# Attention with a max of three products: later differences over blocks of the units, and the softmax scaled on DVE

## The chip, the cores and the metric

The kernel runs on one core of one Trainium2 chip. The metric is device microseconds (us) of one execution. A measurement is repeated, and the median of the runs is given. The engines are TensorE (PE, with its weight loads shown apart as PEld), VectorE (DVE), ScalarE (ACT), GpSimd (POOL) and SyncE (SP). Each works through its own queue in order, and waits for the others by semaphores. DMAs are issued from the queues of SP, ACT and POOL.

## The reference, cut to what matters

```python
batch, n_heads, seq, head_dim = (8, 8, 576, 64)
scores = scale * np.matmul(q, k.transpose(0, 1, 3, 2))
mask = (rel >= 0) & (rel < 128)                      # a window of 128 keys
scores = np.where(mask, scores + bias[None], -1000000000.0)
attn = np.exp(scores - np.max(scores, axis=-1, keepdims=True))
attn = attn / (np.sum(attn, axis=-1, keepdims=True) + 1e-09)
x = np.matmul(attn, v)                               # to 4608 tokens x 512
h = np.maximum(np.maximum(x @ w1, x @ w2), x @ w3)   # 512 -> 768, three times
out = h @ w_out                                      # 768 -> 512
```

All is float32.

## The kernel before

**Attention.** A task is one batch entry and one pair of heads; there are 32 tasks, four to a batch entry. Each goes in five steps of 128 queries (the last has 64), and the steps are taken in pairs. For a pair, `products` makes the scores on PE, `score` folds the window by a predicated copy on DVE, adds the bias and takes the least value on DVE (L289), and takes the exponential on ACT (L293), which leaves the sum of each row. `sums_of` adds 1e-9 (L302) and takes the reciprocal (L305), both on DVE and on two or four values per row. `normalise` then multiplies each 128x128 tile of the exponentials by the reciprocal of its row: four instructions for a pair of steps, two for a single one, on ACT (L312). `turn` transposes the tiles on PE (L321), ACT copies them out of PSUM (L325, L331, L334), POOL cuts two triangles (L335, L339), and `mix` multiplies by v (L361).

**The units.** The products with the weights are done as a fast matrix multiplication of 2x2 blocks by 2x2 blocks: seven products (`unit(u)`, taken in the order k = 0, 1, 6 of the group before, 2, 3, 4, 5) in place of eight. A batch entry has eleven groups of seven: nine with w1, w2, w3 (g = 0 to 8) and two with w_out (g = 9 and 10). Each operand is split into a high and a low part in float32r, and three of the four products of the parts are made, so a unit has 6 matmuls for g < 9 and 18 for g >= 9 (L510). A unit ends with a copy out of PSUM on ACT (`t`, L519) or with `put`, which adds two parts (L473, L476) and takes the maximum (L468, L474) into the tiles `hq` on DVE. Three banks of PSUM take turns.

**The differences over blocks.** Three groups make one third p of the hidden layer: four blocks b00, b01, b10, b11 in `hq`. The products with w_out need the blocks and four differences: t = b01 - b00, t' = b11 - t, b01' = b11 - b01 and b10' = b10 - t'. `factors_h` issues these (`sub`, on DVE, L391) and the splits of the results (`cut`: the high part is a copy on ACT, L387, the low part a subtraction on POOL, L388, or on DVE for two of them at p = 2). The differences are written in place, over `t`, b01 and b10. So t' waits until POOL has made the low part of t, and b10' waits until POOL has made the low part of b10.

**The order.** `later(when, what, ...)` puts a piece of work on a list, and unit number `when` issues it ahead of its own matmuls. Before, the work that a `put` of unit u calls for is issued at u + 1: for block (0,0) the splits of b00 and t; for (1,1) t', b01' and the splits of t' and b11; for (1,0) the splits of b01' and b10, then b10' and its split. The events of attention, units and the preparing of the weights are sorted by hand-written times (`at`); `normalise` stands 0.4 steps behind `sums_of`, and `turn` of that pair comes about two and a half steps later. Within one engine the trace shows small exchanges against the order of the code: at 419.94 us b01' runs ahead of t' at 421.17 us.

**The weights.** In the first 200 us or so DVE and ACT also prepare the weights (L136 to L169), and SP stores them to HBM (L171). After that POOL issues DMAs that stream them back for every batch entry, through a ring of two places (L221).

Of the kernel before, what the change touches and what calls it, by code (L numbers as in the profile page):

```python
# [12 lines left out]
AF = mybir.ActivationFunctionType  # L13
ALU = mybir.AluOpType
# [15 lines left out]
def attention_maxout_kernel(  # L30
# [11 lines left out]
    nc = tc.nc  # L42
# [43 lines left out]
        out=prev, in_=prev, pattern=[[1, P]], compare_op=ALU.is_gt, fill=0.0,  # L86
# [220 lines left out]
    def normalise(t, i):  # L307
        n = rows[i]
        st, two = stats[t, i // 2]
        for a, p in enumerate(two):  # L310
            for j in range(2):
                nc.scalar.activation(p[:n, j], p[:n, j], AF.Copy, scale=st[:n, 2, a, j:j + 1])  # L312

    def turn(s):
        pt = ps_t.tile([P, 2, 2, P], F32, name="pt")
# [63 lines left out]
    def later(when, what, *args):  # L379
        todo.append((when, what, args))  # L380
        todo.sort(key=lambda x: x[0])
# [3 lines left out]
    def split(out, src, e):  # L385
        hi, lo = out
        nc.scalar.copy(out=hi, in_=src)  # L387
        e.tensor_tensor(out=lo, in0=src, in1=hi.bitcast(F32), op=ALU.subtract)  # L388

    def sub(out, x, y):  # L390
        nc.vector.tensor_tensor(out=out, in0=x, in1=y, op=ALU.subtract)  # L391
# [28 lines left out]
    def factors_h(b, p, ij, when):  # L420
        b00, b01, b10, b11 = [hq.get((p, x)) for x in ((0, 0), (0, 1), (1, 0), (1, 1))]

        def cut(k, src):
            if p < 2:
                if p == 0:
                    hs[b, k] = hs_p.tile([P, 2, 2, C], F32R, name="hs")
                t = hs[b, k][:, p]
            else:
                if k in (0, 2, 4, 5):
                    hs[b, "at"] = hs_p.tile([P, 2, 2, C], F32R, name="hs2", bufs=4)  # L430
                t = hs[b, k, 2] = hs[b, "at"][:, k in (1, 3, 6)]
            split((t[:, 0], t[:, 1]), src, nc.vector if p == 2 and k < 2 else nc.gpsimd)

        if ij == (0, 0):
            t = hq["t", p] = t_p.tile([P, C], F32, name="t")
            sub(t, b01, b00)
            later(when, cut, 0, b00)
            later(when, cut, 1, t)
        elif ij == (1, 1):
            t = hq["t", p]  # L440
            later(when, sub, t, b11, t)
            later(when, sub, b01, b11, b01)
            later(when, cut, 2, t)
            later(when, cut, 3, b11)
        elif ij == (1, 0):
            t = hq["t", p]
            later(when, cut, 5, b01)
            later(when, cut, 4, b10)
            later(when, sub, b10, b10, t)
            later(when, cut, 6, b10)  # L450

    def put(b, g, ij, ps, e, when):
        i, j = ij
        if g >= 9:
            o = t_p.tile([P, C], F32, name="t")
            if e is None:
                nc.scalar.copy(out=o, in_=ps)
            else:
                nc.vector.tensor_tensor(out=o, in0=ps, in1=e, op=ALU.add)
            m = i * W + (g - 9) * P  # L460
            nc.sync.dma_start(outT[m:m + P, b * S + j * C:b * S + (j + 1) * C], o)
            return
        p, w = divmod(g, 3)
        if w == 0:
            hq[p, ij] = hq_p.tile([P, C], F32, name="hq")
        h = hq[p, ij]
        if w and e is None:
            nc.vector.tensor_tensor(out=h, in0=ps, in1=h, op=ALU.max)  # L468
        elif e is None:
            nc.scalar.copy(out=h, in_=ps)  # L470
        elif w:
            s = t_p.tile([P, C], F32, name="t")
            nc.vector.tensor_tensor(out=s, in0=ps, in1=e, op=ALU.add)  # L473
            nc.vector.tensor_tensor(out=h, in0=s, in1=h, op=ALU.max)  # L474
        else:
            nc.vector.tensor_tensor(out=h, in0=ps, in1=e, op=ALU.add)  # L476
        if w == 2:
            factors_h(b, p, ij, when + 1)
# [54 lines left out]
    for t, (b, hp) in enumerate(tasks):  # L533
        for i in range(NB):
            s = t * NB + i + shift[b]
            if i == LOAD_I and t + 2 < len(tasks):
                at(s - 0.4, load, t + 2)
            if i == NB - 1 and t + 1 < len(tasks):
                at(s - 0.4, load_v, t + 1)
            if i == 0 and 0 < t < NP:  # L540
                at(s - 1, slopes, t)
            c = s - (t * NB + i) % 2

            if s == c:
                at(c + LAG_T + 0.02, turn, t * NB + i)
                at(c + 0.03, products, t * NB + i)
            at(s + 0.04, score, t, i)
            if i % 2 or i + 1 == NB:
                at(s + 0.9, sums_of, t, i)
                at(s + 1.3, normalise, t, i)  # L550
            e = t * NB + next(min(e + 1, NB - 1) for e in GROUPS if e >= i)
            at(e - e % 2 + shift[b] + LAG_X + 0.01, mix, t, i)

    ready = [n_steps * (b + 1) - 2 + LAG_X + 0.05 + shift[b] for b in range(B)]
    when = ready[0]
    for b in range(B):
# [4 lines left out]
        for u in range(77 * b, 77 * b + 77):  # L561
            if u == 77 * b + 63 and b + 1 < B:
                when = max(when, ready[b + 1])
# [53 lines left out]
```

## Time and profile before

| | us |
|---|---|
| median of 3 runs (lowest, highest) | 849.85 (846.66, 851.54) |
| the profiled execution's own time | 846.03 |
| its span, first to last instruction | 844.3 |
| PE busy | 780.3 (92% of the span) |
| PEld busy | 674.3 (80%) |
| DVE busy | 570.0 (68%) |
| ACT busy | 544.5 (64%) |
| POOL busy | 310.3 (37%) |

The profiled execution is one of many: it is 3.8 us below the median of the runs. The shares are means over very different stretches. In the first 190 us attention for the first two batch entries and the preparing of the weights go side by side. From there to about 740 us a pattern repeats about every 94 us: the products of one batch entry and the attention for the next. After 740 us only products are left. A row of groups of instructions gives the line, the engine, the operation, out<-in with shapes, the count, the busy time and the mean of one in ns, and then the engine's idle time ahead of them with what ended it. In a timeline the columns are the start, the duration, the engine, the line, and in brackets how long the engine had been idle and what ended that.

### The profile page before, as it was taken

Reading aid. Unit: us, or ns where it says so; the run is one execution under the profiler, and the core shown is the slowest. Engines: PE = TensorE matmul, PEld = TensorE weight load, DVE = VectorE, ACT = ScalarE, POOL = GpSimd, SP = SyncE. Lnnn points to the kernel's source line nnn. Section 1 sums busy time; section 2 is a strip of 40 time slices with the busy share of each in tenths; the row PEclk is TensorE's granted clock in tenths of the full one; section 3 lists DMA queues with packets and bytes.
Section 4 is the critical chain, followed back from the end, with each engine's and each line's share of the span. In section 5 each row is a group of like instructions: output and inputs, shape, how many; then the busy total and the mean of one; then the engine's idle time right before and its main releaser. Section 6 shows DMA issues by size and latency. Waiting matters only on the chain.

```text
span 844.3 us, 17942 instructions
## 1 busy us (share of the span) xinstructions
PE 780.3 (92%) x6272; PEld 674.3 (80%) x6272; DVE 570.0 (68%) x1830; ACT 544.5 (64%) x1790; POOL 310.3 (37%) x544
## 2 busy tenths in 40 slices
PE   4767778799999999999999999999999999999997
PEld 2335666589888988888888988889888988889897
DVE  5788989996666845775557845775657846583552
ACT  6898888876666856676556756675657756642332
POOL 1212141442354415452345415451345415440431
PEclk9865989799999999999999999999999999999999
DMA  6742568673887558873787558873787557764851
GB/s 230 278 168 70 220 230 305 210 257 125 262 277 249 195 171 261 277 253 118 239 273 252 196 175 267 275 255 110 245 281 240 194 187 244 230 223 153 296 205 56
DMA packets 43401, 184.78 MB, mean 219 GB/s; under 512 B 4784, under 2 KB 13744, under 8 KB 34096
## 3 DMA queue, kind: packets, MB, share of 16 engines
q0 software_dynamic: 18144, 115.61, 41.7%
q1 hardware_dynamic: 25024, 67.97, 22.8%
q8 instruction: 49, 0.80, 0.4%
q14 instruction: 40, 0.33, 0.1%
q10 hardware_dynamic: 144, 0.07, 0.0%
HBM read 157.68 MB, written 25.95 MB: 217 GB/s over the span
## 4 chain that ended last, share of the span: by engine, by line
PE 68%; DVE 8%; issue 8%; POOL 6%; ACT 6%; DMA 3%; SPq 0%; POOLq 0%; ACTq 0%; DVEq 0%
PE ps_m L510 53%; PE ps_x L361 6%; PE ps_s L259 5%; PE pt L321 4%; POOL hs L388 3%; DMA wt<-keep 2%; POOL pp L339 1%; POOL pp L335 1%; ACT p L293 1%; ACT hs L387 1%; DVE hs L158 1%; DVE t L473 1%; DMA hs<-in_w_all 1%; DVE hs L144 1%; DVE xs L388 1%
## 5 line engine op out<-in xcount | busy, mean ns | idle before, releaser
L510 PE MATMUL ps_m<-xs,wt 128*128 128x288 f32 x3024 | 440.8, 302 | 19.9 <-DVE hq L476 7.6
L510 PEld LDWEIGHTS ps_m<-xs,wt 128*128 128x128 f32 x3024 | 414.6, 191 | 46.6 <-issue 12.2
L519 ACT COPY t<-ps_m 128x288 f32<-128x288 f32 x264 | 101.2, 392 | 92.3 <-PE ps_m L510 91.9
L335 POOL TENSOR_SCALAR_AFFINE_SELECT pp<-pr 128x256 f32<-128x256 f32 (+1 forms) x128 | 53.9, 421 | 263.0 <-ACT pr L334 175.9
L510 PE MATMUL ps_m<-hs,ow 128*128 128x288 f32 x1008 | 144.5, 299 | 3.2 <-POOL hs L388 2.4
L293 ACT ACTIVATE p<-s,st 128x128 f32<-128x128 f32 (+1 forms) x320 | 126.7, 399 | 27.9 <-DVE st L289 27.2
L510 PEld LDWEIGHTS ps_m<-hs,ow 128*128 128x128 f32 x1008 | 136.0, 188 | 9.6 <-POOL hs L388 5.9
L388 POOL TENSOR_TENSOR hs<-hq,hs 128x288 fp32r<-128x288 f32 x112 | 101.3, 914 | 88.3 <-ACT hs L387 88.1
L221 POOL DMA_DIRECT2D wt<-keep x126 | 69.8, 554 | 150.3 <-PE ps_m L510 148.8
L312 ACT ACTIVATE p<-p,st 128x128 f32<-128x128 f32 (+1 forms) x320 | 108.6, 399 | 20.6 <-DVE st L305 20.0
L289 DVE CUSTOM_DVE_ANT_0 s<-ps_s,bias 128x128 f32<-128x128 f32 (+1 forms) x300 | 77.5, 283 | 25.9 <-PE ps_s L259 19.0
L473 DVE TENSOR_TENSOR t<-ps_m,t 128x288 f32<-128x288 f32 x144 | 65.1, 453 | 43.5 <-PE ps_m L510 27.3
L361 PE MATMUL ps_x<-pp,v 128*64 128x256 f32 (+3 forms) x768 | 85.6, 338 | 7.3 <-POOL pp L335 6.6
L277 DVE COPY_PREDICATED ps_s<-prev,ps_s 128x256 f32<-128x256 uint8 x120 | 50.6, 421 | 56.9 <-PE ps_s L259 55.7
L259 PE MATMUL ps_s<-qk 64*64 64x192 f32 (+1 forms) x1080 | 71.3, 346 | 11.5 <-DVE st L289 7.4
L321 PE MATMUL pt<-ident,p 128*128 128x128 f32 (+1 forms) x320 | 62.0, 295 | 17.3 <-ACT p L312 15.2
L387 ACT CAST hs<-hq 128x288 fp32r<-128x288 f32 x120 | 50.3, 433 | 39.0 <-DVE hq L474 26.0
L361 PEld LDWEIGHTS ps_x<-pp,v 128*64 128x64 f32 (+1 forms) x768 | 46.7, 140 | 35.1 <-POOL pp L335 11.8
L321 PEld LDWEIGHTS pt<-ident,p 128*128 128x128 f32 (+1 forms) x320 | 37.2, 145 | 42.7 <-ACT p L312 20.9
L474 DVE TENSOR_TENSOR hq<-t,hq 128x288 f32<-128x288 f32 x144 | 67.4, 475 | 2.7
L259 PEld LDWEIGHTS ps_s<-qk 64*64 64x64 f32 x1080 | 40.1, 141 | 26.9 <-issue 13.2
L293 ACT ACTIVATION_READ_ACCUMULATOR p<-s,st 128x1 f32 (+1 forms) x320 | 61.5, 192 | 0.0
(56 smaller groups left out, 719.2 us busy)
## 6 DMA issues: line engine op xcount, KB each, us to landing
wt<-keep POOLq DMA_DIRECT2D x63, 1024.0 KB, 7.2
wt<-keep POOLq DMA_DIRECT2D x63, 768.0 KB, 4.6
qk<-in_qk SPq DMA_DIRECT2D x31, 576.0 KB, 5.8
hs<-in_w_all SPq DMA_DIRECT2D x24, 512.0 KB, 6.6
v<-in_v SPq DMA_DIRECT2D x32, 320.0 KB, 4.8
keep<-wt SPq DMA_DIRECT2D x9, 1024.0 KB, 4.7
outT<-t SPq DMA_DIRECT2D x64, 144.0 KB, 1.8
keep<-wt SPq DMA_DIRECT2D x9, 768.0 KB, 5.2
```

What stands on the lines that cost most here:

```text
L221: nc.gpsimd.dma_start(wts[n, a], keep[n % 9][a])
L259: nc.tensor.matmul(ps[j][d:d + D, o:o + k1 - k0], lhsT=qkt[t][j * D:(j + 1) * D, 0, q0:q0 + D], rhs=qkt[t][j * D:(j + 1) * D, 1, k0:k1], s ...
L289: nc.vector.tensor_tensor_reduce(out=s[:n], in0=ps[j][:n, P:2 * P], in1=(bias if i else bias0)[:n, 2 * hp + j, :], scale=-0.125, scalar=3. ...
L293: nc.scalar.activation(p[:n, j], s[:n], AF.Exp, bias=st[:n, 0, a, j:j + 1], scale=-1.0, accum_out=st[:n, 1, a, j:j + 1])
L312: nc.scalar.activation(p[:n, j], p[:n, j], AF.Copy, scale=st[:n, 2, a, j:j + 1])
L321: nc.tensor.transpose(out=pt[:, a, j, :n], in_=p[:n, j], identity=ident[:n, :n])
L361: nc.tensor.matmul(x[j * D:(j + 1) * D, c:c + e - a], lhsT=vv[:n, i, j * D:(j + 1) * D], rhs=w[:n, j].rearrange("p a b -> p (a b)")[:, a:e ...
L388: e.tensor_tensor(out=lo, in0=src, in1=hi.bitcast(F32), op=ALU.subtract)
L473: nc.vector.tensor_tensor(out=s, in0=ps, in1=e, op=ALU.add)
L474: nc.vector.tensor_tensor(out=h, in0=s, in1=h, op=ALU.max)
L510: nc.tensor.matmul(ps, lhsT=lt, rhs=rt, start=i == 0 and k in (0, 1, 4), stop=i == len(pairs) - 1, skip_group_check=True,)
L519: nc.scalar.copy(out=e, in_=ps)
```

## The change

```
@@ normalise
-                nc.scalar.activation(p[:n, j], p[:n, j], AF.Copy, scale=st[:n, 2, a, j:j + 1])
+                nc.vector.tensor_scalar(
+                    out=p[:n, j], in0=p[:n, j], scalar1=st[:n, 2, a, j:j + 1], scalar2=None, op0=ALU.mult
+                )
@@ factors_h
         elif ij == (1, 1):
             t = hq["t", p]
+            when += 2 * (p < 2)
             later(when, sub, t, b11, t)
             later(when, sub, b01, b11, b01)
             later(when, cut, 2, t)
...
             later(when, cut, 5, b01)
             later(when, cut, 4, b10)
-            later(when, sub, b10, b10, t)
-            later(when, cut, 6, b10)
+            later(when + 5, sub, b10, b10, t)
+            later(when + 5, cut, 6, b10)
```

The multiplication by the reciprocal goes from ACT to DVE, with the reciprocal as one value per partition. For p = 0 and 1 the differences t' and b01' and the splits of t' and b11 are issued at u + 3 in place of u + 1. For all p the difference b10' and its split are issued five units later, at u + 6 in place of u + 1. The amount of work is the same.

More of the change, by code (lines that the diff above doesn't have):

```diff
@@ L311, in normalise @@
             for j in range(2):
-                nc.scalar.activation(p[:n, j], p[:n, j], AF.Copy, scale=st[:n, 2, a, j:j + 1])
+                nc.vector.tensor_scalar(
+                    out=p[:n, j], in0=p[:n, j], scalar1=st[:n, 2, a, j:j + 1], scalar2=None, op0=ALU.mult
+                )
     def turn(s):
@@ L440, in factors_h @@
             t = hq["t", p]
+            when += 2 * (p < 2)
             later(when, sub, t, b11, t)
@@ L448, in factors_h @@
             later(when, cut, 4, b10)
-            later(when, sub, b10, b10, t)
-            later(when, cut, 6, b10)
+            later(when + 5, sub, b10, b10, t)
+            later(when + 5, cut, 6, b10)
     def put(b, g, ij, ps, e, when):
```

## The prediction

> **What bounds the kernel now.** I read the mean clock and span first, then the busy time by stretches, then who waited for whom on PE in each stretch, and last the timeline around the longest waits. The table of stretches gives PE, PEld, DVE, ACT and POOL busy (with counts), then the granted PE clock, the DMA share and GB/s:
>
> ```profile
> 10.00:75.00 65.00, 44.13 (x282) 21.61 (x283) 53.87 (x214) 58.86 (x200) 14.68 (x32) 0.74 0.56 204
> 75.00:195.00 120.00, 100.80 (x730) 82.22 (x729) 113.42 (x340) 97.88 (x299) 35.89 (x55) 0.87 0.62 223
> 195.00:740.00 545.00, 535.83 (x4526) 476.10 (x4527) 348.79 (x1163) 349.06 (x1192) 226.00 (x403) 1.00 0.68 225
> 740.00:844.30 104.30, 96.24 (x708) 92.83 (x704) 51.23 (x105) 34.67 (x87) 31.40 (x45) 1.00 0.55 187
> ```
>
> Four stretches have four limits. From 10 to 75 us ACT is busy 91% and DVE 83%, and PE waits for both. From 75 to 195 us DVE is busy 94.5%: it is the limit. From 195 to 740 us PE is busy 98%, so only its few waits can be won. At the end it is products and DMAs. The waits of PE and PEld from 200 to 750 us (total, times, longest):
>
> ```profile
> PE ps_m L510 <- DVE hq L476: 7.0, 5, 1.4
> PE ps_m L510 <- POOL hs L388: 1.0, 5, 0.2
> PE ps_m L510 <- ACT t L519: 0.9, 1, 0.9
> PEld ps_m L510 <- DVE hq L476: 8.2, 5, 1.6
> ```
>
> One wait makes nearly all of it: five times 1.4 us, on DVE's `put`. The timeline shows what it is:
>
> ```profile
> 425.11 1.54 POOL L388 TENSOR_TENSOR hs<-hq,hs 128x288 fp32r<-128x288 f32 x2
> 426.68 0.46 DVE L391 TENSOR_TENSOR hq<-hq,t 128x288 f32<-128x288 f32 x1 [1.61 <-POOL hs L388]
> 427.06 0.82 DVE L476 TENSOR_TENSOR hq<-ps_m,t 128x288 f32<-128x288 f32 x2
> 427.18 0.43 ACT L387 CAST hs<-hq 128x288 fp32r<-128x288 f32 x1 [1.28 <-DVE hq L391]
> 427.57 3.46 PE L510 MATMUL ps_m<-xs,wt 128*128 128x288 f32 x24 [1.40 <-DVE hq L476]
> ```
>
> b10' writes over b10, so it stands on DVE until POOL has split b10 (425.11 + 1.54 = 426.65). Two `put`s stand behind it on DVE, and PE has no free bank until they are done.
>
> **The change, part by part.** First the differences. With b10' five units later, at some 0.8 us a unit (24 matmuls in 3.46 us are four units), it is issued 4 us later; POOL was done 1.6 us after DVE began to wait, so the wait goes. t' two units later, 1.6 us, likewise gives POOL time for t. Nothing is added: the same instructions, no DMA, no new wait; the blocks are overwritten much later and the first reader of their splits, a product with w_out, is tens of units on for p < 2. For p = 2 b10' is issued ahead of the second unit of group 10 and its split is read late in the third: a unit of 18 matmuls lasts some 2.5 us at that rate, against 0.46 on DVE, 0.43 on ACT and 0.8 on POOL. That covers it. What is late next on PE is POOL's 0.2 us waits, which stay. Gain: five times 1.40 (PE) to 8.2 in all (PEld), I take 7.5. The single wait of 0.9 on ACT's copy follows a difference t' that took 2.01 us on DVE, and ACT has less to do: another 0.9.
>
> ```profile
> 254.32 2.01 DVE L391 TENSOR_TENSOR t<-hq,t 128x288 f32<-128x288 f32 x1
> ```
>
> **-8.4 us**, bounds -9.5 and -6.
>
> The same wait shows at the end, but PE's bracket there names something else:
>
> ```profile
> 791.07 1.09 PEld L510 LDWEIGHTS ps_m<-xs,wt 128*128 128x128 f32 x8 [1.14 <-DVE hq L476]
> 791.10 1.16 PE L510 MATMUL ps_m<-xs,wt 128*128 128x288 f32 x7 [0.94 <-DMA wt<-keep]
> 782.32 8.65 DMA wt<-keep
> 801.44 7.58 DMA wt<-keep
> ```
>
> The last two rows are from the chain that ended last: without attention PE runs up to the stream of weights. A free bank is no use before the weights land. **-0.5**, bounds -2 and 0.
>
> Now the scaling. The old and the nearest new prices, by groups (shapes apart), and where the old ones lie (ACT busy by stretch, of L312 alone):
>
> ```profile
> L312 ACT ACTIVATE p<-p,st 128x128 f32<-128x128 f32 x256 | 86.0, 398 | 6.8 <-DVE st L305 6.2
> L312 ACT ACTIVATE p<-p,st 64x128 f32<-64x128 f32 x64 | 23.3, 400 | 13.8 <-DVE st L305 13.8
> L141 DVE TENSOR_SCALAR hs<-hs 128x512 int32<-128x512 int32 x24 | 10.4, 452 | 0.0
> 10.00:75.00 65.00, 13.39 (x40) 0.74 0.56 204
> 75.00:195.00 120.00, 15.03 (x44) 0.87 0.62 223
> 195.00:740.00 545.00, 80.23 (x236) 1.00 0.68 225
> ```
>
> No scaling of 128 elements is in the trace of DVE. Its two neighbours are:
>
> ```profile
> 42.21 0.75 DVE L141 TENSOR_SCALAR hs<-hs 128x512 int32<-128x512 int32 x2
> 136.57 0.42 DVE L141 TENSOR_SCALAR hs<-hs 128x512 int32<-128x512 int32 x1
> 443.43 0.15 DVE L302 TENSOR_SCALAR st<-st 128x4 f32<-128x4 f32 x1
> 443.50 0.28 DVE L289 CUSTOM_DVE_ANT_0 s<-ps_s,bias 64x128 f32<-64x128 f32 x1
> 443.71 0.45 DVE L391 TENSOR_TENSOR t<-hq 128x288 f32<-128x288 f32 x1
> ```
>
> Four elements hold DVE for 0.07 us (443.43 to 443.50), 512 for 0.33 (0.75 less 0.42). Between these, 128 elements take 0.07 + 124 x 0.26 / 508 = 0.13. From above, L289 on 128 elements per partition holds it for 0.21 (443.50 to 443.71). I take 0.14, nearer the same operation; bounds 0.13 and 0.21. The Trainium skill, "VectorE: DVE Perf Modes", section "The perf-mode tier table", gives a float32 tensor_scalar in SBUF two elements a cycle; the 0.26 us for 508 elements are 0.51 ns each, which is that.
>
> From 75 to 195 us: 44 x 0.14 = 6.2 us more on an engine that has 6.6 us idle in 120, and 15 us less on ACT. PE's and DVE's waits for ACT there:
>
> ```profile
> PE ps_m L510 <- ACT t L519: 5.1, 3, 4.3
> PE pt L321 <- ACT p L312: 4.8, 5, 3.1
> DVE wt L169 <- ACT wt L168: 2.1, 4, 1.0
> ```
>
> The 2.1 us of DVE's should mostly go; PE's help only where PE is what DVE waits for, which is rare here. **+4**, bounds -4 (PE's waits halved, scalings in DVE's gaps) and +13 (the price of 0.21, 9.2, and a few holds behind POOL, below).
>
> From 10 to 75 us: 40 x 0.14 = 5.6 on DVE gives 59.5 of 65, and ACT falls from 58.9 to 45.5. The two change places, and the wait below is likely to shrink, since the scaling then follows its reciprocal on the same engine:
>
> ```profile
> PE pt L321 <- ACT p L312: 10.4, 4, 4.2
> ```
>
> **-2**, bounds -8 and +5.6.
>
> From 195 to 740 us: 236 x 0.14 = 33 us on DVE, 64% busy, become 70%. The scalings of a pair stand 0.55 us in front of `put`s. That they cost PE little is shown by holds that are there already:
>
> ```profile
> 427.70 0.80 POOL L388 TENSOR_TENSOR hs<-hq,hs 128x288 fp32r<-128x288 f32 x1 [0.52 <-ACT hs L387]
> 427.79 0.73 DVE L302 TENSOR_SCALAR st<-st 64x2 f32<-64x2 f32 x1
> 446.98 3.31 DVE L302 TENSOR_SCALAR st<-st 64x2 f32<-64x2 f32 x1
> 447.96 2.30 POOL L388 TENSOR_TENSOR hs<-hq,hs 128x288 fp32r<-128x288 f32 x3
> 463.12 0.55 POOL L221 DMA_DIRECT2D wt<-keep  x1 [1.91 <-PE ps_m L510]
> 463.54 0.17 DVE L302 TENSOR_SCALAR st<-st 128x4 f32<-128x4 f32 x1 [0.22 <-ACT p L293]
> ```
>
> A tensor_scalar that meets POOL's subtraction is held until POOL's run of them ends: 0.73 and 3.31 us in place of 0.16. Neither hold is followed by a wait of PE above 0.4 us, the second because PE has the transposes and score products of attention to do meanwhile. Beside POOL's DMA issue there is no hold (0.17). Some of the twelve calls of `normalise` a batch entry will meet such runs: by the row of L388 alone (DVE and POOL busy), POOL is in them 18% of the stretch:
>
> ```profile
> 195.00:740.00 545.00, 34.65 (x46) 98.85 (x110) 1.00 0.68 225
> ```
>
> So some waits of PE appear: **+2**, bounds 0 and +14 (two holds a pattern that reach PE at 1.4, five patterns).
>
> The Trainium skill, "SBUF — State Buffer", section "SBUF: two separate sides", says that a DVE op in a two-port mode and a GpSimd op hold the shared pair of ports exclusively, and that the loser "fully blocks". The rows above agree (3.31 us). By that rule each of the 320 scalings would also hold back POOL's descriptors for the weights; the 0.55 us issue beside L302 shows no such thing for four elements, and no row has it for 128.
>
> The sum: -8.4 - 0.5 + 4 - 2 + 2 = -4.9 us. Against the profiled execution's own 846.0 (844.3 of span and 1.7 around it) that is 841.1; the median of the runs stands 3.8 higher, so **845.0 us**.
>
> **The rivals.** (a) *Given back*: the removed wait comes again in another place. One hold of the scalings behind POOL's run in each pattern reaches PE at 1.4 us, as b10' did, so +7 in place of +2, and -4.9 becomes 0: 849.9. For it: the 3.31 us hold recurs in each pattern, and the later splits keep POOL's run as long. Against it: that hold costs PE nothing now. It is also the time if small exchanges of order bring the differences back to where they were. This is where the page's exclusive ports would take the time.
>
> (b) *Slower*: the preparing of the weights, 10 to 195 us, is bound by DVE throughout. 84 scalings at 0.14 are 11.8 us; 21 or so calls, of which a quarter meet a run of POOL at some 0.7, make 4; with the rest of the sum (-8.4, -0.5, +2) this is +8.9: 858.7. It decides from the point where over 11 us of DVE's added time reach the end. For it: 94.5% busy. Against it: ACT is 28 us freer in that stretch and both engines wait for each other.
>
> (c) *More*: ACT, not DVE, sets the pace in the preparing. If the 10.4 + 4.8 + 5.1 us of PE's waits for ACT go by half and the scalings fit in gaps, the two stretches give -8 in place of +2: 835. For it: ACT's 91% ahead of 75 us. Against it: DVE's 94.5% behind it.
>
> **How the numbers follow.** A measurement of this kernel can tell about 0.5%, 4.2 us, from no change. The forecast, -4.9 with its own range from 841 to 848, has 0.37; (a) 0.30; (b) 0.21; (c) 0.12. Faster is the forecast and (c), 0.49; within 0.5% is (a), 0.30; slower is (b), 0.21. The range holds (c) nearly and (b) in part: 836 to 857.
>
> **What would show it.** In the new profile the five waits of PE for L476 near 1.4 us are gone and no DVE L391 waits over 1 us for POOL; if they stand, the first step is wrong. The scaling shows 320 times on DVE with a median near 0.22 us shown (0.14 held), and a few at 0.7 to 3 us. The busy share of DVE in the stretch that ends where PE becomes full, and the time at which it does (195 us now), decide between the forecast, (b) and (c). New waits of PE for `put`s or transposes after 195 us, at places where a scaling is long, would show (a). The prediction is wrong above all if the end of the preparing moves by more than 6 us either way.

## The result and the profile after

The changed kernel takes **876.89 us** (median; 872.85 to 879.59) against 848.80 for the kernel before in the same session: a ratio of 1.0325 with a 95% interval of 1.0271 to 1.0379. It is 28 us slower, where 4.9 us faster had been forecast. The profiled execution took 872.85 us, 871.2 of them span.

The busy time of each engine, with its share of the span and its count:

```profile
PE 786.6 (90%) x6272; PEld 676.1 (78%) x6272; DVE 640.0 (73%) x2150; ACT 458.6 (53%) x1470; POOL 323.7 (37%) x544
```

The table of stretches, cut at the same places of the work as the prediction's (columns as there):

```profile
10.00:83.00 73.00, 42.37 (x274) 21.21 (x276) 58.92 (x248) 49.06 (x159) 16.61 (x32) 0.68 0.50 178
83.00:215.00 132.00, 106.61 (x749) 84.89 (x742) 122.94 (x385) 86.67 (x256) 42.04 (x56) 0.91 0.57 203
215.00:766.00 551.00, 539.35 (x4524) 476.08 (x4524) 405.28 (x1402) 284.15 (x957) 231.63 (x401) 1.00 0.68 224
766.00:871.20 105.20, 94.59 (x699) 91.77 (x697) 50.15 (x103) 34.69 (x87) 31.08 (x45) 1.00 0.55 180
```

The first two stretches were 65 and 120 us long and are now 73 and 132. That is 20 of the 28 us, in the stage where the weights are prepared. ACT has 9.8 and 11.2 us less to do there. Here is the same stage, up to the copy of task 8's output, first in the kernel before, then in the changed one, and then in a later experiment that scales the early tasks on POOL (PE, PEld, DVE, ACT, POOL busy, clock, DMA):

```profile
10.00:220.30 210.30, 170.23 (x1219) 126.94 (x1220) 180.94 (x605) 171.59 (x553) 56.03 (x98) 0.85 0.59 210
10.00:240.90 230.90, 173.34 (x1217) 127.85 (x1216) 199.35 (x703) 146.43 (x454) 63.18 (x98) 0.84 0.54 190
10.00:252.30 242.30, 182.27 (x1215) 132.91 (x1208) 180.65 (x603) 151.85 (x473) 122.66 (x178) 0.76 0.51 182
```

In the changed kernel DVE is busy 18.4 us longer and idle 2.2 us longer: most of the 20.6 us is DVE's own time. The third row says that this is not the only way to lose it: there DVE has no more to do than before, and the stage is 32.0 us longer. The granted clock of PE does not explain the loss either: it is 0.85 before and 0.84 in the changed kernel, and in the traced execution of the changed kernel with the weights first (below) it is 0.96, with the same delay of task 8 (+20.9).

The scaling's group (busy, mean ns | idle before), and from the timeline a run of four with the instruction behind it (start, length shown, engine and line):

```profile
L312 DVE TENSOR_SCALAR p<-p,st 128x128 f32<-128x128 f32 x256 | 81.8, 368 | 1.1
```

```profile
50.15 0.87 DVE L312 TENSOR_SCALAR p<-p,st 128x128 f32<-128x128 f32 x4
50.93 0.43 DVE L277 COPY_PREDICATED ps_s<-prev,ps_s 128x256 f32<-128x256 uint8 x1
```

Four of them keep DVE for 50.93 - 50.15 = 0.78 us, 0.195 each; the mean of 0.368 is the length shown, which overlaps the next instruction, with the held ones in it. The prediction took 0.14, with 0.21 as its upper bound.

What PE waits for, up to 240 us (total, times, longest), and then from 241 to 770 us:

```profile
PE ps_x L363 <- POOL pp L337: 15.1, 14, 2.8
PE pt L323 <- DVE p L312: 14.2, 6, 6.2
```

```profile
PE ps_m L513 <- POOL hs L390: 4.5, 5, 0.9
PE ps_m L513 <- DVE st L305: 2.1, 3, 0.7
PE ps_m L513 <- DVE hq L479: 1.4, 2, 0.7
PE ps_m L513 <- ACT t L522: 0.9, 1, 0.9
PE pt L323 <- DVE p L312: 0.3, 1, 0.3
```

Early, PE waits for p about as long as before (15.2 us for ACT then), and more than twice as long for the selects on POOL behind it:

```profile
PE pt L321 <- ACT p L312: 15.2, 9, 4.2
...
PE ps_x L361 <- POOL pp L335: 6.6, 7, 2.3
```

These are the rows of the kernel before, up to 220.3 us. After 241 us the five waits of 1.4 us for `put` have gone, and five waits of 0.9 us for POOL's low parts and smaller ones for DVE stand in their place: 9.2 us now, 8.9 before. PE's busy time from task 8 to task 31 also grew, from 519.4 to 522.6 us, which no run here explains.

The five waits of 0.9 us are for the split of b10' at p = 2. It is made late, two selects are ahead of its low part on POOL, and PE is ready before it:

```profile
501.97 0.45 DVE L393 TENSOR_TENSOR hq<-hq,t 128x288 f32<-128x288 f32 x1
...
503.00 0.92 POOL L341 TENSOR_SCALAR_AFFINE_SELECT pp<-pr 128x256 f32<-128x256 f32 x1
503.89 0.79 POOL L390 TENSOR_TENSOR hs<-hq,hs 128x288 fp32r<-128x288 f32 x1
504.73 0.53 PE L513 MATMUL ps_m<-hs,ow 128*128 128x288 f32 x2 [0.89 <-POOL hs L390]
```

With the differences alone, or the scaling alone, PE has no such wait of 0.9 us: it takes both parts of the change. For p = 0 the timeline shows b10' (L393) and the `put`s (L479) around it:

```profile
447.22 1.56 POOL L390 TENSOR_TENSOR hs<-hq,hs 128x288 fp32r<-128x288 f32 x2
...
447.33 0.45 DVE L479 TENSOR_TENSOR hq<-ps_m,t 128x288 f32<-128x288 f32 x1
...
448.82 0.46 DVE L393 TENSOR_TENSOR hq<-hq,t 128x288 f32<-128x288 f32 x1 [0.78 <-POOL hs L390]
449.19 0.45 DVE L479 TENSOR_TENSOR hq<-ps_m,t 128x288 f32<-128x288 f32 x1
...
449.63 0.43 DVE L479 TENSOR_TENSOR hq<-ps_m,t 128x288 f32<-128x288 f32 x1
...
449.70 0.95 PEld L513 LDWEIGHTS ps_m<-xs,wt 128*128 128x128 f32 x7 [0.95 <-DVE hq L479]
```

Five products later in the code became one `put` later on DVE: b10' now has one ahead of it and still two behind it, and still waits for POOL, 0.78 us in place of 1.61.

### The profile page after: what moved, and what is told of

The parts are those of the page before. It is cut to its first block, busy times and chain, and to the rows that moved or that the text cites. A ratio compares the mean times of both kernels' runs of the same rounds, so it can differ in the third digit from the quotient of the medians.

```text
span 871.2 us, 17921 instructions
## 1 busy us (share of the span) xinstructions
PE 786.6 (90%) x6272; PEld 676.1 (78%) x6272; DVE 640.0 (73%) x2150; ACT 458.6 (53%) x1470; POOL 323.7 (37%) x544
## 4 chain that ended last, share of the span: by engine, by line
PE 52%; DVE 15%; POOL 12%; issue 12%; ACT 4%; DMA 4%; SPq 0%; POOLq 0%; ACTq 0%; DVEq 0%
PE ps_m L513 40%; POOL hs L390 6%; PE ps_x L363 5%; PE ps_s L259 4%; PE pt L323 3%; POOL pp L341 3%; DVE p L312 3%; POOL pp L337 3%; DMA wt<-keep 3%; DVE hq L477 2%; DVE t L476 1%; DVE hq L393 1%; DVE s L289 1%; ACT p L293 1%; DVE ps_s L277 1%
## 5 line engine op out<-in xcount | busy, mean ns | idle before, releaser
L522 ACT COPY t<-ps_m 128x288 f32<-128x288 f32 x264 | 103.3, 395 | 127.1 <-PE ps_m L513 125.3
L337 POOL TENSOR_SCALAR_AFFINE_SELECT pp<-pr 128x256 f32<-128x256 f32 (+1 forms) x128 | 61.9, 483 | 283.2 <-ACT pr L336 174.0
L513 PE MATMUL ps_m<-hs,ow 128*128 128x288 f32 x1008 | 146.6, 300 | 8.2 <-POOL hs L390 7.1
L363 PE MATMUL ps_x<-pp,v 128*64 128x256 f32 (+3 forms) x768 | 90.0, 338 | 15.6 <-POOL pp L337 15.1
L312 DVE TENSOR_SCALAR p<-p,st 128x128 f32<-128x128 f32 (+1 forms) x320 | 101.8, 364 | 1.5
L363 PEld LDWEIGHTS ps_x<-pp,v 128*64 128x64 f32 (+1 forms) x768 | 48.5, 142 | 45.6 <-POOL pp L337 20.4
L477 DVE TENSOR_TENSOR hq<-t,hq 128x288 f32<-128x288 f32 x144 | 70.1, 493 | 2.2
L341 POOL TENSOR_SCALAR_AFFINE_SELECT pp<-pr 128x256 f32<-128x256 f32 (+1 forms) x128 | 65.3, 510 | 0.0
```

What stands on the lines that cost most here:

```text
L312: nc.vector.tensor_scalar(out=p[:n, j], in0=p[:n, j], scalar1=st[:n, 2, a, j:j + 1], scalar2=None, op0=ALU.mult)
L337: nc.gpsimd.affine_select(out=pp[t, i - 1][:, :, 1, :n], in_=r[:, a, :, :n], pattern=[[0, 2], [-1, n]], compare_op=ALU.is_gt, fill=0.0, ba ...
L341: nc.gpsimd.affine_select(out=w[:n, :, 0, :n], in_=r[:n, a, :, :n], pattern=[[0, 2], [1, n]], compare_op=ALU.is_ge, fill=0.0, base=0, chan ...
L363: nc.tensor.matmul(x[j * D:(j + 1) * D, c:c + e - a], lhsT=vv[:n, i, j * D:(j + 1) * D], rhs=w[:n, j].rearrange("p a b -> p (a b)")[:, a:e ...
L513: nc.tensor.matmul(ps, lhsT=lt, rhs=rt, start=i == 0 and k in (0, 1, 4), stop=i == len(pairs) - 1, skip_group_check=True,)
L522: nc.scalar.copy(out=e, in_=ps)
```

## The experiments

To see where the time arises, the start of ACT's copy of each task's output (`xk<-ps_x`, L370 before) is compared with the kernel before, in the profiled executions. Here are those of tasks 3, 8 and 31, at 71.6, 220.3 and 748.9 us before. Up to task 8 kernels that do the same work differ by up to 3.7 us (the one without moved differences in batch entry 0), so these columns read to some 4 us. The traced execution of the kernel before is also some 3 us faster than its median, which makes most entries a little too large; the medians are safer for sums. From task 8 to task 31 the traces are steadier: 528.6 to 529.1 us in the eight kernels whose work there is that of the kernel before.

| kernel | median us | ratio, 95% interval | task 3 | task 8 | task 31 |
|---|---|---|---|---|---|
| changed | 876.89 | 1.0325 (1.0271 to 1.0379) | +7.8 | +20.5 | +24.7 |
| scaling alone | 874.58 | 1.0291 (1.0254 to 1.0329) | +7.9 | +21.6 | +27.1 |
| differences alone | 850.41 | 1.0005 (0.9991 to 1.0020) | +0.1 | +6.6 | +3.0 |
| scaling from task 8 on | 861.98 | 1.0137 (1.0103 to 1.0171) | 0 | +7.1 | +12.1 |
| scaling up to task 7 | 867.89 | 1.0225 (1.0179 to 1.0270) | +8.1 | +20.0 | +18.0 |
| unused scalings on DVE | 857.87 | 1.0100 (1.0075 to 1.0125) | +2.3 | +13.2 | +13.4 |
| scaling by a constant | 873.44 | 1.0290 (1.0263 to 1.0317) | +2.6 | +15.3 | +26.6 |
| low parts on POOL | 850.17 | 1.0008 (0.9989 to 1.0027) | +3.4 | +2.9 | +3.1 |
| differences, not batch entry 0 | 846.81 | 0.9970 (0.9951 to 0.9988) | +2.1 | +3.7 | +0.3 |
| the same, b10' by eight | 846.42 | 0.9963 (0.9940 to 0.9986) | -0.1 | +1.3 | -2.0 |
| changed, scaling sooner | 879.36 | 1.0361 (1.0329 to 1.0392) | +6.2 | +26.0 | +33.9 |
| early scaling on POOL | 878.32 | 1.0326 (1.0285 to 1.0368) | +12.9 | +32.0 | +32.3 |
| before, weights later | 851.04 | 1.0015 (0.9999 to 1.0030) | +2.0 | +2.2 | +2.4 |
| changed, weights first | 874.28 | 1.0273 (1.0244 to 1.0302) | +11.2 | +20.9 | +27.6 |
| before, weights first | 847.73 | 0.9974 (0.9957 to 0.9991) | +1.0 | +1.4 | +1.9 |
| changed, weights later | 874.05 | 1.0275 (1.0258 to 1.0291) | +6.8 | +21.0 | +26.2 |
| eight columns on DVE | 861.81 | 1.0142 (1.0105 to 1.0180) | +4.3 | +15.3 | +15.4 |
| early scaling, ACT as loaded | 869.18 | 1.0226 (1.0187 to 1.0265) | +4.0 | +23.3 | +23.6 |
| best of the parts | 844.59 | 0.9931 (0.9903 to 0.9959) | +0.6 | -0.4 | -2.9 |

### Which part, and in which stage

*Scaling alone* is the first hunk of the diff without the others, *differences alone* the others without the first. The next two are the changed kernel with the scaling split by task, with this condition and with `t < 2 * NP`:

```diff
+                if t >= 2 * NP:
+                    nc.vector.tensor_scalar(...)
+                else:
                     nc.scalar.activation(p[:n, j], p[:n, j], AF.Copy, scale=st[:n, 2, a, j:j + 1])
```

> The scaling on DVE, the differences as before. Theory A (the scalings lengthen the stretch in which the weights are prepared, where DVE sets the pace, and the differences do next to nothing because DVE still meets b10' at the same place): within 5 us of the changed kernel, some 872 to 881 us, with the preparing ending near 193 us as there, and the wait of 1.6 us for b10' back. Rival B (the later differences cost the time, by the order of work on all engines): close to the kernel before, under 860 us.

> The later differences, the scaling on ACT as before. Theory A: within 6 us of before (843 to 855 us), most likely a little faster if some of the five waits of 1.4 us go. Rival B: slower than before by more than half of the 28 us, over 862 us. The forecast's term of -8.4 us would give 840 us.

> The changed kernel, but the scaling of the first eight tasks (the preparing) stays on ACT; from the ninth task on it is on DVE. Theory A: about 20 of the 28 us go, some 852 to 858 us, and the ninth task's output is copied near 220 us as before. Rival C (the scalings cost about the same in every batch entry, by holds behind POOL): only a quarter of the 28 us goes, about 870 us.

> The reverse: the scaling of the first eight tasks is on DVE, from the ninth on it is on ACT. Theory A: 865 to 875 us, the ninth task's output near 240 us as in the changed kernel, and afterwards a pattern of 94 us or less. Rival C: about 857 us.

The scaling alone makes 25.3 us of the loss, the differences nothing that can be told from zero. The scaling of the first eight tasks makes most of it, 18.6 us by the medians, and has done so by task 8. From task 8 to 31 the changed kernel loses 4.2 us, and with the early scaling alone it wins 2.0: the late scaling costs 6.2 us there. It is 8.6 us where the early scaling stays on ACT, and 5.5 without the moved differences. By the medians it is more, 9.0 and 11.6 us, and the scaling from task 8 on took 862 us where 852 to 858 had been expected. The differences alone lose 6.6 us by task 8 and win 3.6 after it. With the scaling on DVE their loss by task 8 does not show (+20.5 against +21.6).

### What the early scaling costs

Two theories: DVE sets the pace of the preparing and each us added to it is a us lost; or the wait of the transposition on DVE's queue makes the loss. Against the first stands a rival of its own, that only the price was wrong. *Unused scalings* leaves the work on ACT and adds, for t < 2 * NP,

```diff
+                    nc.vector.tensor_scalar(
+                        out=dist[:n], in0=dist[:n], scalar1=warm[:n], scalar2=None, op0=ALU.mult
+                    )
```

and *scaling by a constant* has `scalar1=0.0625` in place of the row's reciprocal, so it leaves the division by the row's sum out.

> The kernel before, its scaling on ScalarE as it was, with one more per-partition scaling of 128x128 on VectorE beside each of the first eight tasks' (88 of them, of a constant tile by a column of ones, the result not used). Theory A (VectorE's time sets the pace of the preparing, one for one): 88 x 0.20 = 17.6 us appear by task 8 though ScalarE has not one instruction less and no transposition waits for the new ones; the output copy of task 8 comes 15 to 20 us later, 864 to 869 in all, about what the scaling of those eight tasks alone gave (867.9). Rival B (what costs is the dependence: the transpositions wait for a scaling at the end of VectorE's queue): nothing waits for these, so at most the 18 us of idle time that VectorE has in that stage fills up, 849 to 854.

> All scalings on VectorE, differences as before, but by one constant in the instruction instead of the row's own reciprocal (the division by the row's sum is left out). If an operand per partition is what makes it one element a cycle, four in a row fall from 0.87 to about 0.6 and each holds the engine for 0.14: at the same rate per us of VectorE the loss of 25 us shrinks to 0.14/0.20 of it, 17 to 18 us, 866 to 868. If it is the operation's own speed in any form, the rows stay at 0.87 for four and the time at 873 to 876.

The first of these adds 80 instructions, not 88 (times shown: least, median, most), of about 0.195 us on DVE as above:

```profile
L314 DVE TENSOR_SCALAR dist<-dist,warm x80: 265/276/876, 3.1 to 188.3; 128x128 f32<-128x128 f32 x64, 64x128 f32<-64x128 f32 x16
```

So 80 x 0.195 = 15.6 us of DVE's time, which no transposition waits for (the making of the bias from `dist` waits once, 1.6 us), cost 857.87 - 849.14 = 8.7 us: 0.56 us for each, 0.41 to 0.68 by the interval. That is neither theory's number: it counts, but some half of it is hidden.

With the constant, four scalings and the instruction behind them are:

```profile
45.37 0.62 DVE L312 TENSOR_SCALAR p<-p 128x128 f32<-128x128 f32 x4
45.91 0.41 DVE L277 COPY_PREDICATED ps_s<-prev,ps_s 128x256 f32<-128x256 uint8 x1
```

0.54 us for four, 0.135 each: the price that the prediction had taken. Yet the kernel takes 873.4 us. By task 8 it is 5.2 us better than the changed kernel and 6.3 better than the scaling alone, about what 80 x 0.06 = 4.8 us of DVE give; after task 8 it loses more (11.3 us in place of 5.5). Its scalings need no reciprocal, and DVE now stands waiting for the exponential in front of them (busy, mean | idle before):

```profile
L312 DVE TENSOR_SCALAR p<-p 128x128 f32<-128x128 f32 (+1 forms) x320 | 86.3, 291 | 12.4 <-ACT p L293 11.5
```

A right price would not have saved the forecast.

Two later runs separate what is left. *Eight columns* gives 8 of the 128 columns of each early tile to DVE and the rest to ACT; *ACT as loaded* is the early scaling on DVE with a useless scaling of `dist` by ones on ACT beside each:

```diff
+                c = 8 * (t < 2 * NP)
+                if c:
+                    nc.vector.tensor_scalar(out=p[:n, j, :c], in0=p[:n, j, :c], ...)
+                nc.scalar.activation(p[:n, j, c:], p[:n, j, c:], AF.Copy, ...)
```

> The kernel before, with 8 of the 128 columns of each tile of the first eight tasks scaled on VectorE and the other 120 on ScalarE: the transposition now waits for VectorE's queue as in the changed kernel, but VectorE gets 80 short instructions (of some 0.07 us by the 0.15 to 0.17 us of L302 with its start) and ScalarE keeps its work. If the dependence on VectorE's queue makes the 10 us that its time does not explain: 856 to 861. If it does not: 849 to 853, the 80 x 0.07 = 5.6 us at the rate of the unused scalings (8.7 us for 16) being 3 us.

> The scaling of the first eight tasks on VectorE, and ScalarE makes as many scalings of a constant tile by ones in their place, the results not used (differences as before). If ScalarE's relief is what does harm (its queue comes early to copies that wait for PE, and the weights' steps stand behind them), some 8 to 10 us of the 20 come back though work was only added: 857 to 861. If the relief does nothing, 867 to 870; if it had given something, more than 871.

The short scalings were not short:

```profile
31.06 0.62 DVE L314 TENSOR_SCALAR p<-p,st 128x8 f32<-128x8 f32 x4
31.59 0.41 DVE L277 COPY_PREDICATED ps_s<-prev,ps_s 128x256 f32<-128x256 uint8 x1
```

0.53 us for four, 0.133 each, so this run added 80 x 0.133 = 10.6 us to DVE and lost 11.4. It doesn't show the dependence without the time, as it was meant to. But beside the others it gives a price: **in the chain from the exponential to the product with v, a us of DVE's time costs 1.1 us (11.4 / 10.6; 0.84 to 1.44 by the interval) to 1.2 us (18.7 / 15.6, early scaling with ACT as loaded; 1.02 to 1.44); beside the chain 0.56.** The price in the chain holds the time on DVE and the longer chain together; these runs don't part the two. And ACT's relief was worth nothing that they can tell: against the kernel before in its own session, the early scaling cost 18.6 us with it (there with the differences moved, whose median is 1.1 us off) and 18.7 without, each to some 4 us.

### Other places for the scaling and for the load

*Scaling sooner* is the changed kernel with one time changed:

```diff
-                at(s + 1.3, normalise, t, i)
+                at(s + 0.95, normalise, t, i)
```

*Early scaling on POOL* is the kernel before with `nc.gpsimd.tensor_scalar` for t < 2 * NP; *low parts on POOL* is the kernel before with L169 on `nc.gpsimd` for odd k.

> The changed kernel with normalise due right behind sums_of (0.05 of a step instead of 0.4 later). Of the 20 us that the scaling cost by task 8, VectorE's time alone gave 8.7 us (the unused scalings), so 10 to 12 would be the coupling: transpositions that wait for a scaling queued late on VectorE, ScalarE's copies behind them, and VectorE's own next step behind those. If the scaling's place in VectorE's queue makes these waits, PE's 14 us for p become less than half and the time 866 to 872. If the waits are there wherever it is queued (the scaling waits for the sum of the row just before), or other waits come in their place, 874 to 879.

> The kernel before, the scaling of the first eight tasks on GpSimd instead of ScalarE: VectorE gets nothing more, ScalarE is relieved as in the changed kernel. If ScalarE's relief is worth what VectorE's load costs, this shows it without the load: 840 to 846. If relief of ScalarE is worth nothing there, 848 to 851 where GpSimd keeps up; and if GpSimd is slow with it or VectorE holds it (a select of 0.40 us took up to 3.04 us beside VectorE's weight steps), the chain from the exponential to the product with v grows by it: 855 to 870.

> The kernel before, with the low parts of every other block of the weights' preparing subtracted on GpSimd instead of VectorE. Theory A run the other way: VectorE is relieved of 36 subtractions in the preparing, so task 8's output should come earlier by a good part of what they took, 5 to 12 us, 838 to 845 in all. Rival: GpSimd is slower for it and shares VectorE's port (3.8 us beside it for what takes 0.87 alone), the split blocks come late, 850 to 865.

Sooner was no better, and PE's waits for p were 16.0 us in place of 14.2, so the hand-written due time is not what makes them. On POOL a scaling takes 0.68 us at the median, and PE waits for it:

```profile
L313 POOL TENSOR_SCALAR p<-p,st x80: 592/684/3781, 15.0 to 204.6; 128x128 f32<-128x128 f32 x64, 64x128 f32<-64x128 f32 x16
```

```profile
PE pt L326 <- POOL p L313: 35.9, 33, 6.0
```

DVE has nothing added here (180.7 us busy by task 8, 180.9 before), ACT is relieved, and task 8 is 32 us late: a longer chain alone can cost this much, here with POOL's selects behind the scalings in one queue. Moving 36 of DVE's subtractions to POOL won nothing either. It is a weak test of DVE's load, because DVE's busy time by task 8 fell by 1.7 us only (180.9 to 179.2): POOL takes about twice as long for them, and what stays on DVE gets slower beside it. These are DVE's subtractions and sums in the kernel before, then POOL's subtractions and DVE's groups in this one (busy, mean ns):

```profile
L169 DVE TENSOR_TENSOR wt<-hs,wt 128x256 fp32r<-128x256 f32 x63 | 26.8, 443 | 2.3 <-ACT wt L168 2.1
...
L158 DVE TENSOR_TENSOR hs<-hs 128x256 f32<-128x256 f32 x36 | 15.9, 448 | 0.0
```

```profile
L170 POOL TENSOR_TENSOR wt<-hs,wt 128x256 fp32r<-128x256 f32 x27 | 23.3, 866 | 39.1 <-ACT wt L168 38.2 <-DVE st L290 0.8
```

```profile
L170 DVE TENSOR_TENSOR wt<-hs,wt 128x256 fp32r<-128x256 f32 x36 | 19.2, 539 | 2.4 <-ACT wt L168 2.4
L158 DVE TENSOR_TENSOR hs<-hs 128x256 f32<-128x256 f32 x36 | 17.6, 491 | 0.0
```

### A theory that the runs don't bear out

The chain of waits of the changed kernel shows a ring of in-order queues (start, length, what):

```profile
70.65 3.05 POOL pp L337
...
73.74 1.98 PE ps_x L363 x8
75.72 0.42 PE pt L323 x2
...
76.23 0.37 ACT pr L336
76.61 0.57 ACT hs L140
...
77.20 0.78 DVE hs L144
```

A select of 0.40 us lasts 3.05, a product and a transposition wait behind it on PE, ACT's copy of that transposition waits, the weights' tanh (L140) stands behind the copy, and DVE's next weight step waits 3.78 us for the tanh by the timeline. To break the link of the tanh, `at(s + 0.2, weights, 2)` became `s - 0.1` (ahead of the transpositions) or `s + 0.6`, in both kernels:

> The changed kernel with the steps of the weights' preparing issued ahead of the transpositions of each step instead of behind them. What is open is the 10 us by task 8 that VectorE's time does not explain. Ring theory: ScalarE's copy of a transposition heads its queue while the transposition waits for VectorE's scaling (or for a select and a product behind it), and the weights' tanh behind that copy holds VectorE's next weight step (3.78 us at 77.20 us, nine of such waits' us in all). With the tanh ahead of the copy that link is gone: VectorE's waits for it fall from 9 to under 3 us and 4 to 10 us come back, 867 to 873. If the loss is only that the chain from the exponential to the product with v is longer over VectorE, nothing comes back: 875 to 880.

> The kernel before with the same place of the weights' steps, as a control. Its ScalarE has no wait of over 1.5 us between 30 and 112 us, so the ring has nothing to give there: 847 to 852. If it gains as much as the changed kernel does, the place of the weights is worth something of its own and says nothing on the ring.

> The changed kernel with the weights' steps 0.4 steps later, which left the kernel before as it was (851.0). By the ring theory the place of the tanh against the copies counts here although it did not there: 868 to 873 where it falls ahead of the next copies, 879 to 885 where the waits become longer. If the changed kernel is as indifferent to it as the one before, 875 to 879.

> The kernel before with the steps of the weights' preparing issued 0.4 steps later in each step; same instructions, other order. If only the amount of work of the engine that sets the pace counts in the preparing, 847 to 851. If the order counts (on whose in-order queue a wait stands, which select on GpSimd falls beside a burst of the weights on VectorE), task 8's output moves by 4 us and more in either direction, and nothing after it: 840 to 845 or 853 to 860.

In the changed kernel DVE waits 8.9 us for the tanh up to 240 us. Here is that wait with the weights ahead of the transpositions, and then with them later (total, times, longest):

```profile
DVE hs L144 <- ACT hs L140: 9.5, 4, 3.8
```

```profile
DVE hs L144 <- ACT hs L140: 4.4, 5, 1.7
```

The first edit did not shorten the wait, so it does not test the link. With the second the wait is halved and task 8 is where it was (+21.0), but another wait for ACT has come in its place: that of the low parts (L169) for ACT's copies of the weights (L168) grew from 1.9 to 5.4 us. The ring is there. Its link over the tanh alone is not what costs; whether a ring over all of ACT's steps does, these two runs don't tell. The kernel before is as good as indifferent to the order of the weights' steps (847.7 and 851.0).

### The differences

*Not batch entry 0* moves them only for b > 0, that is from the second batch entry on (the second block of rows of the expectations); *b10' by eight* does so with 8 in place of 5 for p = 0 and 1; the *best* is the latter with `s - 0.1` for the weights.

```diff
+            when += 2 * (p < 2 and b > 0)
...
-            later(when, sub, b10, b10, t)
+            later(when + 5 * (b > 0), sub, b10, b10, t)
```

> The later differences for the second block of rows on alone, scaling on ScalarE. The moved differences cost 6.6 us by task 8 and won back 2.8 to 3.6 after it. If the loss is made where the first results' differences fall into the preparing, it is gone and the gain stays: 845 to 847. If the loss has to do with anything else of the change, 849 to 851.

> The later differences for the second block of rows on, as in the run before this one, with b10' eight products later instead of five for p = 0 and 1. With five, b10' went back by one or two puts only and five waits of 1.40 became 0.6 and less, 3.5 us in all. If the place of b10' is what is left, the put waits still there between 224 and 749 us (1.9 us of PE) go: 844 to 846. If the result is then late where it is used (the units with w_out), the waits for hs take them over: 847 to 851.

> Neither part's loss: scaling on ScalarE, the differences of the second block of rows on later (846.4 alone) and the weights' steps ahead of the transpositions (847.7 alone). If the two gains have different places (after and ahead of task 8), they add: 843.5 to 845.5. If both are of the same order of chance, 846 to 849.

Without batch entry 0 the 6.6 us by task 8 are gone but for what the table can't tell (+3.7 and +1.3), and the gain of 3.4 us after it stays. PE's waits for DVE between 223 and 749 us, with five and with eight products:

```profile
PE ps_m L511 <- DVE hq L477: 1.9, 3, 0.6
PE ps_m L511 <- DVE st L305: 1.3, 2, 0.6
```

```profile
PE ps_m L511 <- DVE st L305: 2.5, 4, 0.6
...
PE ps_m L511 <- DVE hq L477: 0.6, 1, 0.6
```

The further move took the waits for `put` and gave as much to the reciprocal (L305) that stands in front of the next `put`: 3.2 us became 3.1. What is late next after b10' is that, and not POOL's 0.2 us. The best version takes 844.6 us, 0.7% below the kernel before.

## Why the prediction was wrong, by its steps

**The preparing: +4 and -2.** This is the step that failed. The two terms together stood for +2 and measured about 20 (task 8), far beyond the 6 us that the prediction itself had named as the sign of being wrong above all. The later stretch is 12 us longer, inside its bounds of -4 and +13; the first one, for which -2 was forecast, is 8 us longer, outside its bounds of -8 and +5.6. The price was one part: 0.195 in place of 0.14, 4.6 us on 84 scalings. The larger part is the set-off. The prediction took 6.2 and 5.6 us on DVE and paid for them with PE's waits for ACT and with "15 us less on ACT". Giving ACT its load back changed nothing that can be told, and DVE's time came through at 1.1 to 1.2. PE's wait for p in the first stretch, which was "likely to shrink" with the reciprocal and the scaling on one engine, grew from 10.4 to 13.9 us. In the later stretch it went from 4.8 us to nothing, and the stretch became longer all the same. Rival (b), "bound by DVE throughout", came nearest, at 0.21, and the prediction had the row that speaks for it, 94.5% busy. Its formula gives 84 x 0.195 + 4 = 20.4 us, against some 20, but that the numbers meet is partly luck. The 4 us of holds behind POOL were about 1.4 (the 80 early scalings held DVE 17.0 us in the changed kernel), and DVE's time beside the chain cost only 0.56, so the stage is not bound by DVE alone.

**The price of 0.14.** Both neighbours that it was drawn between have constants in them. The scaling by a constant confirms that line: 0.135. The operand per partition adds 0.06, and no tensor_scalar before had one. The value from above, 0.21, was the nearer one.

**The differences: -8.4.** Right mechanism, mis-sized: in their own stage they gave 3.4 to 3.6 us. "Issued 4 us later" was counted in products; on DVE it was one or two `put`s, so b10' still waited for POOL. "What is late next on PE is POOL's 0.2 us waits" left out the reciprocal. "That covers it", said of p = 2, held for the differences alone but not beside the scaling, where PE waits 0.9 us five times. And that "nothing is added" did not hold for batch entry 0, whose differences fall into the preparing and cost up to 6.6 us there; how, the runs leave open.

**The tail: -0.5.** Not to be told: from the last output copy to the end it is 95.4 us before, 97.6 after, and 94.8 to 100.0 in the experiments.

**195 to 740 us: +2.** Measured 5.5 to 8.6 in the traces and 9.0 to 11.6 by the medians, within the bounds of 0 and 14. In the changed kernel it cancels the differences' gain, as rival (a) had it: 8.9 us of PE's waits became 9.2. The way is not that of rival (a), though: scalings are held for some 3.4 us behind POOL's runs (3.38 at 373.06 us), but PE waits only 0.3 us for one. The time came by the late split at p = 2 and by waits for the reciprocal and `put`s.

The errors add up, as far as the traces can tell: 18 for the preparing, 9 for the differences and the tail, which together gave nothing, and 4 to 7 for the rest make 31 to 34, against the 33 us between -4.9 and +28.1.

**Open** is which link makes DVE's time in the chain dearer than beside it. The due time and ACT's relief are excluded by runs, the tanh alone is unlikely. That the select on POOL is held beside DVE's weight steps is seen, but was not taken away; with eight columns on DVE, PE's waits for the selects stayed at 7.5 us (6.6 before) and DVE's time still cost 1.1.

## What to carry to other kernels

Before an operation moves to an engine that is busy 94% of a stage, ask whether it stands in the chain of that stage: there its time counted in full here, and the relief of the other engine was worth nothing. A due time in the code is not a place in an engine's queue: count by how many instructions of that queue the moved one goes back, and what then stands in front of the next. Move such work only where the limiting engine has room: here the differences paid once batch entry 0 was left alone.

## What the hardware showed unexpectedly

A scaling of 128 elements held DVE 0.195 us with an operand per partition and 0.135 with a constant; with such an operand, 8 elements still took 0.133. From 8 to 128 that is 0.062 us for 120 elements, 0.52 ns each, so the dearer form is not slower per element but has a dearer start. The Trainium skill, "VectorE: DVE Perf Modes", section "The perf-mode tier table", gives two elements a cycle for a float32 tensor_scalar in SBUF: the slope agrees.

A GpSimd select that takes 0.40 us alone took 3.04 us beside DVE's weight steps:

```profile
70.65 3.04 POOL L337 TENSOR_SCALAR_AFFINE_SELECT pp<-pr 128x256 f32<-128x256 f32 x1 [4.80 <-ACT pr L327]
70.87 1.28 DVE L137 SCALAR_TENSOR_TENSOR hs<-hs 128x512 int32<-128x512 int32 x2
...
72.07 0.75 DVE L141 TENSOR_SCALAR hs<-hs 128x512 int32<-128x512 int32 x2
72.74 0.68 DVE L144 TENSOR_TENSOR hs<-hs 128x512 f32<-128x512 f32 x1
73.64 0.40 POOL L341 TENSOR_SCALAR_AFFINE_SELECT pp<-pr 128x256 f32<-128x256 f32 x1
```

The sum of the prediction had counted holds of DVE behind POOL only; here an instruction of POOL lasts for the length of DVE's run beside it.
